# A block product in the second MLP matmul in place of DMA transposes of q and k

## The chip, the cores and the metric

The kernel runs on one core of a Trainium2 chip. A core has a matrix engine (TensorE, PE in the profile; its weight loads are listed apart as PEld), three engines for elementwise work (VectorE = DVE, ScalarE = ACT, GpSimd = POOL), a queue engine that only issues transfers (SyncE = SP), 16 DMA engines, an on-chip memory of 128 partitions (SBUF) and a small accumulator memory in which matmuls put their results (PSUM). Every engine works through its own list of instructions in order; engines wait for each other through semaphores. The metric is the device time of one execution in microseconds; several executions are taken and their median is given. The profile is one of these executions.

## The reference

Local attention with a few global keys and a linear bias on distance, then the real part of a two-dimensional Fourier transform added to its input, a normalisation, and a two-layer MLP added again:

```python
scores = scale * np.matmul(q, k.transpose(0, 1, 3, 2)) + bias      # B=4, H=8, S=768, D=64
scores = np.where(keep, scores, -1e9)                              # local 96, global 8
a = softmax(scores)
x = heads_joined(np.matmul(a, v))                                  # (4, 768, 512)
mixed = np.real(np.fft.fft(np.fft.fft(x, axis=1), axis=2))
u = x + mixed
un = (u - mean(u)) / np.sqrt(var(u) + 1e-6)
ch = np.maximum(un @ w_ch1, 0.0) @ w_ch2                           # 512 -> 2048 -> 512
return u + ch
```

The inputs and the output are fp32. The kernel casts to fp16 for its matmuls.

## The kernel before

**Tiling.** Each batch has 768 rows of 512. Attention goes by head pairs, `n = 4 * b + hp`. After attention the rows of a batch are taken in six residues mod 6, and two residues (256 rows) form a chunk, so there are 12 chunks `c = 3 * b + pr`.

**Stages of one batch.**
1. `load` and `cast_qk` bring q, k of a head pair to SBUF (tiles `qs`; for the first head pairs `hT`) and cast them to fp16 (`qk`).
2. `trans` makes `qkT`, q and k with the head dimension on partitions. For batches 0 and 1 twelve TensorE transposes write a PSUM bank `pt` (L495) and DVE copies it out (L501). For batches 2 and 3 (`b >= XB`) `trans_dma` issues four transposes per head pair from the SP queue (L475); `cast_qk` lays out `qk` in two halves for it (L369, L371).
3. `score` (PSUM `sc`), exponentials on ACT (`er`, L555), the mask product on DVE (`ex`, L570), `av` (`pav`, L662) and its normalisation on DVE (`x`, L681 and L682).
4. `bounce` writes `x` to DRAM and reads it back with rows regrouped (`xr`). Beside it `fold_s` and `fold_d` on DVE (L725 to L794) form sums and differences, which save matmuls in the Fourier transform: this is called the fold below.
5. `y_unit` (PSUM `py`, L814 and L817, copied to `zy`), `mirror` on POOL (`rev`, `ww`), `u_unit` (PSUM `pu`, L895; DVE adds `xr` to make `u`, L914), normalised `un` (L929, L931), and `nt_unit`, which transposes it (`ptu`, L959) into `unT` (L967, L969). From `py` to the first MLP matmul is called the passage below.

**The MLP of one chunk.** `ph_unit` makes a pair of 128-wide blocks of the hidden layer: eight matmuls of 256 columns (L987), and a relu by ACT or DVE into `hT` (L993, L994). There are eight such units to a chunk; `hT` has 16 blocks of 256 rows. `pg_unit` multiplies with `w2`: for each of two row blocks `t`, 16 matmuls of 512 columns (L1010) into one bank `pg`, in four parts of four. DVE multiplies by the row's inverse deviation, adds `u` and writes a tile `ob` (L1021), which SP stores (L1026).

**What sets the order.** The builder has a planner, `Plan`, which keeps a clock per engine and emits instructions one after the other. Elementwise work is announced with the engines that may do it, an estimated duration and what it needs. Four streams feed TensorE: `MIX` (stage 5), `ATT` (stages 2 and 3), `PH` and `PG`. `Plan.run` takes the unit that can start first by its estimates, looking ten units ahead in `MIX` and `ATT` and one ahead in `PH` and `PG`. Once built, the order on each engine is fixed. Numbers of buffers are in `NBUF`; a unit waits until its buffer or its PSUM bank is free. Attention and stage 5 share two double banks (`xx`), the MLP has two banks `ph` and two `pg`.

```python
        pl.run([(MIX, True), (ATT, True), (PH, False), (PG, False)])
```

Of the kernel before, what the change touches and what calls it, by code (L numbers as in the profile page):

```python
# [14 lines left out]
P = 128  # L15


class Plan:
# [7 lines left out]
    SEM = 0.06  # L26
    LAT = {"ACT": 0.14, "DVE": 0.12, "POOL": 0.08}

    def __init__(self):
        self.t = {"PE": 0.0, "ACT": 0.0, "DVE": 0.0, "POOL": 0.0, "SP": 0.7, "DMA": 1.9, "DMA2": 0.0}  # L30
        self.tok = {}
        self.ready = []
        self.pending = []
        self.rings = {}
        self.left = {}
        self.n = 0
# [49 lines left out]
    def emit(self, place):  # L86
# [6 lines left out]
        if dma:  # L93
            q = "DMA2" if eng == "ACT" else "DMA"
            end = self.t[q] = max(self.t[q], end) + dma
        else:
            lat += self.LAT.get(eng, 0.0)
# [4 lines left out]
        if ring is not None:  # L102
            self.rings[ring].append(end + lat)
# [4 lines left out]
    def pe(self, us, after=0.0):  # L108
        end = self.t["PE"] = max(self.t["PE"], after) + us
        return end + 0.15  # L110
# [48 lines left out]
def act(n):  # L159
    return 0.06 + n / 1200.0  # L160


def dve(n):
    return 0.085 + n / 960.0


def dve2(n):
    return 0.075 + n / 1920.0
# [7 lines left out]
def kernel(  # L176
# [23 lines left out]
    XB = 2  # L200
# [59 lines left out]
    def bank(tag, name, dtype=FP32):  # L260
# [4 lines left out]
        if "late" not in early:  # L265
# [5 lines left out]
    NBUF = {"hT": 3, "vs": 2, "qk": 2, "qs": 3, "qkT": 4, "er": 2, "eg": 1, "x": 1, "xr": 1, "zy": 1, "eA": 1,  # L271
            "ww": 1, "rev0": 1, "u": 4, "un": 2, "unT": 2, "ob": 2}
# [19 lines left out]
    w2 = kon.tile([P, NJ, Dm], FP16, tag="w2", name="w2")  # L292
# [15 lines left out]
    TT = {}  # L308

    def load(b, hp, which):  # L310
# [5 lines left out]
        if which == "v" and b == 0:  # L316
# [4 lines left out]
            pl.later([("SP", 0.45, run)], free(vtag, vi), 0.0, [("ld", "v", n)], lat=1.7, dma=1.6)  # L321
        elif which == "v":
# [6 lines left out]
            pl.later([("SP", 0.9, run)], free(vtag, vi) + gate, 0.0, [("ld", "v", n)], lat=1.7, dma=2.67)  # L329
        elif b == 0 and hp < 3:  # L330
            cell = {}

            def run(cell=cell):
                cell[0] = buf("hT", hp, [P, 2, NS, 2 * Dh], FP32, 2)
                for w, src in enumerate((q, k)):
                    qk_dma(cell[0][:, w], src, b, h0)
            pl.later([("SP", 0.9, run)], free("hT", hp), 0.0, [("ld", "qk", n, w) for w in range(2)], lat=1.7, dma=3.2)
            for w in range(2):
                cast_qk(b, hp, w, lambda w=w, cell=cell: cell[0][:, w], ("hT", hp))
        else:  # L340
            for w, src in enumerate((q, k)):
                cell = {}
                i = 2 * (n - 3) + w
# [4 lines left out]
                pl.later([("SP", 0.45, run)], free("qs", i) + gate, 0.0, [("ld", "qk", n, w)], lat=1.7, dma=1.6)  # L348
# [6 lines left out]
    def cast_qk(b, hp, w, src, freed):  # L355
        n = HP * b + hp

        def cast(on):
            if n not in qk16:
                qk16[n] = buf("qk", n, [P, 2, NS, 2, Dh] if b < XB else [P, 2, 2, NP, 2, Dh], FP16, 1)  # L360
            if b < XB:
                d = qk16[n][:, w]
                s = src().rearrange("p (h i) (t d) -> p h (i t) d", h=2, t=2).rearrange("p h j d -> p j h d")
            else:
                for t in range(2):
                    d = qk16[n][:, t, w]
                    s = src().rearrange("p (h i) (t d) -> p t i h d", h=2, t=2)[:, t]
                    if on == "ACT":
                        A(d, s, AF.Copy)  # L369
                    else:  # L370
                        nc.gpsimd.tensor_copy(d, s)  # L371
                return
# [81 lines left out]
    def kg_copies(b, hp):  # L454
        n = HP * b + hp
        for s in range(2):
            def cp(s=s):
                c0 = 16 * (hp % 2) + 8 * s
                nc.gpsimd.tensor_copy(
                    kG[b % 2][64 * s:64 * s + 64, hp, c0:c0 + NG].rearrange("p (j m) -> p j m", j=2),  # L460
                    TT[n][64 * s:64 * s + 64, 1, 0:P].rearrange("p (j m) -> p j m", j=2)[:, :, 0:NG // 2])
            pl.later([("POOL", 0.2, cp)], [("qkT", n)] + ([("gldone", b - 2, hp // 2)] if b > 1 else []), 0.0,
                     [("kG", n, s)], [("free", "qkT", n)], rank=RA(b))

    def trans_dma(b, hp):
        n = HP * b + hp
        done = []

        def xb(a, t):
            if not done:  # L470
                TT[n] = buf("qkT", n, [P, 2, S], FP16, 6)
            done.append(1)
            o = TT[n].rearrange("p w (i a t m) -> p a t (w i) m", a=2, t=2, m=64)[:, a, t]
            i = qk16[n][64 * a:64 * a + 64, t].rearrange("p w i h d -> p (w i h d)")
            nc.sync.dma_start_transpose(o, i)  # L475
        at = [(a, t) for a in range(2) for t in range(2)]
        for x, (a, t) in enumerate(at):
            pl.later([("SP", 1.3, lambda a=a, t=t: xb(a, t))],
                     ([("qk", n, 0), ("qk", n, 1)] + free("qkT", n)) if x == 0 else [("xb", n, x - 1)], 0.0,
                     [("xb", n, x)], lat=0.0, dma=0.01)  # L480
        pl.later([("SP", 0.0, lambda: None)], [("xb", n, 3)], 0.0, [("qkT", n)], [("free", "qk", n)], lat=2.2, dma=0.5)
        kg_copies(b, hp)

    def trans(b, hp):
        if b >= XB:
            return trans_dma(b, hp)
        n = HP * b + hp

        def run(start, ring):
# [17 lines left out]
            kg_copies(b, hp)  # L507
# [128 lines left out]
    def av(b, part, jp):  # L636
# [8 lines left out]
        def run(start, ring):  # L645
# [31 lines left out]
            def norm():  # L677
                if b not in X:
                    X[b] = buf("x", b, [P, NS, Dm], FP16, 4 if b else 5)
# [4 lines left out]
            pl.later([("DVE", 0.09 + dve(128 * nh), norm)], free("x", b), e, [("x", b, hp, jp) for hp in part], CD(b),  # L684
# [6 lines left out]
    def bounce(b):  # L691

        on, eng = ("ACT", nc.scalar) if b else ("SP", nc.sync)
        for half in range(2):
            def wr(half=half):
# [4 lines left out]
                for t in range(2):  # L700
                    eng.dma_start(rows[t], X[b][64 * t:64 * t + 64, :, c])
            pl.later([(on, 1.2, wr)], [("x", b, hp, jp) for hp in (2 * half, 2 * half + 1) for jp in range(NP)] + [("xw", b, 0)][:half], 0.0,
                     [("xw", b, half)], [("free", "x", b)], lat=1.7, dma=2.4 if b else 1.5)

        def rd():
            XR[b] = buf("xr", b, [P, NS, Dm], FP16, 3)
            rows = XD[b].rearrange("(m r) d -> m r d", r=6)
            eng.dma_start(XR[b], rows)
        pl.later([(on, 0.5, rd)], [("xw", b, 0), ("xw", b, 1)] + free("xr", b), 0.0, [("xr", b)], lat=1.7, dma=3.8 if b else 2.4)

    def fold_s(b):
# [3 lines left out]
        for n, (c0, cw) in enumerate(parts):  # L715
# [25 lines left out]
            def f4(c0=c0, cw=cw, cell=cell):  # L741
# [7 lines left out]
                     [("f1", b, n)], [("free", "x", b)] * (2 if len(hps) == HP else 1))  # L749
# [19 lines left out]
    def fold_d(b, needs):  # L769
# [30 lines left out]
        pl.later([("DVE", 0.95 + 1.0, g1)], needs + free("eA", ia) + free("ww", IW(b, NA(b))), 0.0, [("w", b, 0)])  # L800
# [83 lines left out]
    def u_unit(b, pr):  # L884
# [4 lines left out]
        def run(start, ring):  # L889
# [20 lines left out]
            def add():  # L910
                u = UT[c] = buf("u", HP + c, [P, 2, Dm], FP32, 2)
                sm = MV[c] = wk.tile([P, 2, 4], FP32, tag="sm", name=f"sm_{c}", bufs=6)
                for a, rr in enumerate((r0, r1)):
# [5 lines left out]
            pl.later([("DVE", 2 * dve(512) + 0.25, add)], [("xr", b)] + free("u", HP + c), e, [("u", c)],  # L919
                     [("free", "xr", b)] + CD(b), ring=ring)  # L920
# [11 lines left out]
            for a in range(2):  # L932
                pl.later([("ACT", 0.52, lambda a=a: un("ACT", a)), ("DVE", 0.38, lambda a=a: un("DVE", a))],
# [5 lines left out]
            for a in range(2):  # L939
                pl.later([("ACT", 0.62, lambda a=a: square(a))],  # L940
# [36 lines left out]
    def ph_unit(c, jp):  # L977
        needs = [("unT", c), ("w1", jp // 2)] + (free("hT", 3 + c) if jp == 0 else []) + [("CD",)]

        def run(start, ring):  # L980
            if jp == 0:
                HT[c] = buf("hT", 3 + c, [P, NJ, CH], FP16, 2)
# [14 lines left out]

    GP = {}

    def pg_unit(c, t, part):  # L1000
        b, pr = divmod(c, NP)
        rs = PAIRS[pr][t]
        needs = [("h", c, 2 * part), ("h", c, 2 * part + 1), ("w2", part)]

        def run(start, ring):
            if part == 0:
                GP[0] = bank("pg", f"pg_{c}_{t}")
            pg = GP[0]
# [193 lines left out]
```

## Time and profile before

| | |
|---|---|
| median of three runs | 290.23 us (288.24 to 290.87) |
| the profiled execution | 288.24 us, its span 286.4 us |
| mean granted TensorE clock | 0.976 |
| PE busy | 254.1 us (89%), 2340 matmuls |
| DVE busy | 172.2 us (60%), 367 instructions |
| ACT busy | 146.6 us (51%), 247 instructions |
| POOL busy | 53.4 us (19%) |
| chain that ended last | PE 74%, DVE 16%, DMA 3%, ACT 2%, SP queue 2% |
| `ph` matmuls L987 | 768, 94.4 us busy |
| `pg` matmuls L1010 | 384, 91.1 us busy |
| DMA transposes L475 | 32 issues of 1.25 us (median), 3.3 us to landing, between 94.8 and 177.2 us |
| loads of `w2` L1099 | four, issued between 68.7 and 73.6 us, 10.8 us to landing |

How to read it: busy time is the union of an engine's instructions. Matmuls overlap and their ends are modelled, so one matmul of 256 columns lasts 273 ns in the list while the next begins after 0.11 us. In a list of groups a row gives line, engine, operation, output and inputs, shapes and count, then busy time and mean duration, then the engine's idle time before the group and who ended it. In a timeline the columns are start, duration, engine, line, operation, and in brackets the idle time before it with its releaser. In a table of stretches, each engine's busy time is followed by its count of instructions, and after POOL come the granted clock, the DMA share and GB/s.

### The profile page before, as it was taken

The page shows a single profiled execution, that of the slowest core. Times are in us where ns is not written, and L with a number is a line of the kernel's source. Part 1 is how long each engine was busy: PE and PEld are TensorE (multiplying, and loading weights), DVE is VectorE, ACT ScalarE, POOL GpSimd, SP SyncE. Part 2 cuts the span into 40 slices and gives each one's busy share as a digit, 9 for nine tenths or more (in the row PEclk, how much of TensorE's full clock was granted, in tenths as well). Part 3 has the DMA queues.
Part 4 walks back from the last instruction along what each step waited for, and adds up shares of the span by engine and source line. Part 5 has one row for each costly group of instructions (what it writes and reads, how often), then busy time and mean ns, then how long its engine had stood idle before and what let it go on. Part 6 is the DMA issues. An engine that isn't in the chain of part 4 may idle for free.

```text
span 286.4 us, 5852 instructions
## 1 busy us (share of the span) xinstructions
PE 254.1 (89%) x2340; PEld 168.4 (59%) x2340; DVE 172.2 (60%) x367; ACT 146.6 (51%) x247; POOL 53.4 (19%) x122
## 2 busy tenths in 40 slices
PE   1899348899997499999999999699999999999993
PEld 1344236688654267666566446568877677757441
DVE  3247996756679956187158985886895735211121
ACT  2667913999761228378392265589334336324000
POOL 1337004316401061331101004030002120100000
PEclk9999958999999799999999999999999999999999
DMA  7997969999999998839566995100242010010111
GB/s 216 286 295 92 192 129 262 202 199 199 194 208 267 240 258 162 152 108 207 130 180 156 178 277 110 41 3 0 57 108 96 37 39 38 2 73 11 64 73 74
DMA packets 75691, 40.19 MB, mean 140 GB/s; under 512 B 33680, under 2 KB 71824, under 8 KB 75664
## 3 DMA queue, kind: packets, MB, share of 16 engines
q1 hardware_dynamic: 66208, 30.91, 45.4%
q0 software_dynamic: 4224, 4.19, 9.5%
q10 hardware_dynamic: 5232, 4.72, 6.8%
q8 instruction: 18, 0.29, 0.5%
q14 instruction: 9, 0.07, 0.1%
HBM read 31.42 MB, written 9.44 MB: 143 GB/s over the span
## 4 chain that ended last, share of the span: by engine, by line
PE 74%; DVE 16%; DMA 3%; ACT 2%; SPq 2%; issue 1%; POOL 1%; ACTq 0%; DVEq 0%; POOLq 0%
PE ph L987 30%; PE pg L1010 23%; PE sc L532 5%; DVE x L682 3%; DVE u L914 3%; PE py L814 3%; PE pu L895 2%; PE pt L495 2%; PE py L817 2%; PE pav L662 2%; DMA qkT<-qk 1%; DMA ident<-idm 1%; SPq L475 1%; PE ptu L959 1%; PE sc L527 1%
## 5 line engine op out<-in xcount | busy, mean ns | idle before, releaser
L987 PE MATMUL ph<-unT,w 128*128 128x256 f16 x768 | 94.4, 273 | 0.2 <-DVE unT L969 0.2
L1010 PE MATMUL pg<-w,hT 128*128 128x512 f16 x384 | 91.1, 380 | 0.0
L987 PEld LDWEIGHTS <-w 128*128 128x128 f16 x768 | 72.1, 98 | 17.7 <-issue 5.9
L993 ACT ACTIVATE hT<-ph 128x512 f16<-128x512 f32 x60 | 35.8, 597 | 46.0 <-PE ph L987 46.0
L1010 PEld LDWEIGHTS <-hT 128*128 128x128 f16 x384 | 36.5, 98 | 36.0 <-issue 1.3
L1021 DVE SCALAR_TENSOR_TENSOR ob<-pg,sm,u 128x512 f32<-128x512 f32 x24 | 18.0, 748 | 49.6 <-PE pg L1010 48.1
L994 DVE TENSOR_SCALAR hT<-ph 128x512 f16<-128x512 f32 x36 | 24.9, 690 | 17.1 <-PE ph L987 16.8
L555 ACT ACTIVATE er<-sc 128x992 f16<-128x992 f32 (+2 forms) x36 | 32.4, 921 | 2.2 <-PE sc L532 2.0
L570 DVE TENSOR_TENSOR ex<-er,mk 128x992 f16<-128x992 f16 (+2 forms) x36 | 22.6, 635 | 6.1 <-ACT er L555 5.9
L814 PE MATMUL py<-t,ww 128*128 128x256 f16 x48 | 13.2, 327 | 13.1 <-DVE ww L779 13.1
L369 ACT ACTIVATE qk<-qs 128x384 f16<-128x384 f32 x30 | 13.6, 514 | 20.3 <-DVE ww L780 8.0
L863 POOL COPY ww<-zy 128x512 f16<-128x512 f16 x16 | 9.3, 610 | 64.4 <-DVE zy L832 36.0
L532 PE MATMUL sc<-qkT 64*128 64x256 f16 (+1 forms) x192 | 17.7, 273 | 1.6 <-ACT qkT L505 0.7
L929 ACT ACTIVATE un<-u,sm 128x512 f16<-128x512 f32 x15 | 10.5, 717 | 15.5 <-DVE sm L918 15.4
L914 DVE SCALAR_TENSOR_TENSOR u<-pu,xr 128x512 f32<-128x512 f32 x24 | 15.6, 687 | 4.0 <-PE pu L895 3.3
L682 DVE TENSOR_TENSOR x<-pav,rc 128x512 f16<-128x512 f32 (+1 forms) x27 | 17.1, 632 | 0.9
L662 PEld LDWEIGHTS <-ex 128*128 128x128 f16 x352 | 15.2, 97 | 3.1 <-issue 1.1
L662 PE MATMUL pav<-v,ex 128*128 128x65 f16 x352 | 16.4, 193 | 0.5 <-DVE x L682 0.4
L830 ACT ACTIVATE zy<-py 128x1024 f16<-128x1024 f32 (+1 forms) x11 | 9.0, 827 | 14.2 <-PE py L817 10.7
L938 ACT ACTIVATE un<-un 128x512 f16<-128x512 f16 x24 | 14.8, 620 | 1.3 <-PE ptu L959 1.3
L532 PEld LDWEIGHTS <-qkT 64*128 64x128 f16 x192 | 6.2, 95 | 15.0 <-issue 11.2
L814 PEld LDWEIGHTS <-ww 128*128 128x128 f16 x48 | 5.6, 116 | 15.8 <-DVE ww L779 13.7
(95 smaller groups left out, 282.6 us busy)
## 6 DMA issues: line engine op xcount, KB each, us to landing
out_dram<-ob SPq DMA_DIRECT2D x24, 256.0 KB, 2.2
qs<-in_q_dram SPq DMA_DIRECT2D x13, 384.0 KB, 6.3
qs<-in_k_dram SPq DMA_DIRECT2D x13, 384.0 KB, 6.4
vs<-in_v_dram SPq DMA_DIRECT2D x24, 192.0 KB, 6.2
w<-in_moe_w_ch_dram POOLq DMA_DIRECT2D x8, 512.0 KB, 10.8
xd<-x ACTq DMA_DIRECT2D x12, 192.0 KB, 4.2
xr<-xd ACTq DMA_DIRECT2D x3, 768.0 KB, 4.5
u<-in_v_dram SPq DMA_DIRECT2D x4, 384.0 KB, 6.2
```

What stands on the lines that cost most here:

```text
L532: nc.tensor.matmul(pa[:, s, c0:c0 + cw], TT[n][lo:lo + 64, 1, i * P:(i + 1) * P], TT[n][lo:lo + 64, 0, i * P:i * P + cw], start=(b > 0), s ...
L555: A(mine(), cut(pa), AF.Exp, 0.0, 0.125)
L570: VT(o, mine(), m, op=ALU.mult)
L662: nc.tensor.matmul(po[:, jj, hh * 65:(hh + 1) * 65], lhsT, v16[b % 2][:, i, h, 0:65], start=(jp == 0 and a == 0), stop=(a == len(ops) - 1) ...
L682: VT(X[b][:, 2 * jp:2 * jp + 2, first * Dh:(first + nh) * Dh].rearrange("p j (h d) -> p j h d", d=Dh), pv[:, :, :, 0:Dh], rc.to_broadcast( ...
L814: nc.tensor.matmul(o, wr, t1_sb[:, rs, 128:384], start=True, stop=(wi is None))
L914: V.scalar_tensor_tensor(u[:, a].rearrange("p (n r) -> p n r", r=4), pu[:, a].rearrange("p (r n) -> p n r", r=4), 1.0, XR[b][:, rr].rearra ...
L987: nc.tensor.matmul(ph[:, a * CH:(a + 1) * CH], w1[:, d, jb * P:(jb + 1) * P], UNT[c][:, d, :], start=(d == 0), stop=(d == ND - 1))
L993: pl.later([("ACT", act(512), lambda: A(dst, ph, AF.Relu)), ("DVE", dve(512), lambda: V.tensor_scalar_max(dst, ph, 0.0))], [], e, [("h", c ...
L994: ("DVE", dve(512), lambda: V.tensor_scalar_max(dst, ph, 0.0))],
L1010: nc.tensor.matmul(pg, HT[c][:, jb, t * P:(t + 1) * P], w2[:, jb, :], start=(jb == 0), stop=(jb == NJ - 1))
L1021: V.scalar_tensor_tensor(cell[0], pg, MV[c][:, t, 3:4], UT[c][:, t, :], op0=ALU.mult, op1=ALU.add)
```

## The change

Two things are exchanged, and the buffers and the planner's numbers with them.

**Transposes.** `XB`, `trans_dma` and the split layout of `qk` go; all 16 head pairs are transposed on TensorE and copied by DVE.

**Second product.** For each chunk, `hT` (256 rows by 2048) and `w2` (2048 by 512) are cut in two along each axis. The 2 by 2 block product is made from seven products of blocks in place of eight (eight matmuls of 256 columns each). The block sums of `w2` are made once (`w2_sums`), those of `hT` for each chunk (`s_sums`), all on VectorE, some of them in place. The products go to two banks, A and D, in five steps; after each step VectorE multiplies by the inverse deviation and adds the bank to `u`, and the next step continues on the bank (matmuls with no start flag). `u` is stored when all are added; `ob` goes.

**Buffers.** `hT` 3 to 2, `qs` 3 to 2, `ob` gone; `x` and `xr` share one buffer; four buffers `sx` and a constant tile `w2t` are new; `w2` shares a tile with q and k of the third and fourth head pairs. The planner's estimates differ throughout.

```diff
-    SEM = 0.06
-    LAT = {"ACT": 0.14, "DVE": 0.12, "POOL": 0.08}
+    SEM = 0.1
...
-        return end + 0.15
+        return end + 0.06
...
 def act(n):
-    return 0.06 + n / 1200.0
+    return 0.19 + n / 1200.0
 def dve(n):
-    return 0.085 + n / 960.0
+    return 0.15 + n / 960.0
 def dve2(n):
-    return 0.075 + n / 1920.0
+    return 0.16 + n / 1920.0
...
-    NBUF = {"hT": 3, "vs": 2, "qk": 2, "qs": 3, "qkT": 4, "er": 2, "eg": 1, "x": 1, "xr": 1, "zy": 1, "eA": 1,
-            "ww": 1, "rev0": 1, "u": 4, "un": 2, "unT": 2, "ob": 2}
+    NBUF = {"hT": 2, "vs": 2, "qk": 2, "qs": 2, "qkT": 4, "er": 2, "eg": 1, "x": 1, "zy": 1, "eA": 1,
+            "ww": 1, "rev0": 1, "u": 4, "un": 2, "unT": 2, "w2": 1, "sx": 4}
...
     def trans(b, hp):
-        if b >= XB:
-            return trans_dma(b, hp)
...
-    def pg_unit(c, t, part):
...
+    def w2_sums(i):
+        def run():
...
+            VT(w2t[:, 1, k0, :], b22, b12, op=ALU.subtract)
+            VT(b12, b12, b11, op=ALU.subtract)
+            VT(w2t[:, 0, k0, :], b22, b12, op=ALU.subtract)
+            VT(w2t[:, 2, k0, :], b21, w2t[:, 0, k0, :], op=ALU.subtract)
+        pl.later([("DVE", 4 * dve2(1024), run)], [("w2", i), ("w2", 2 + i)], 0.0, [("w2t", i)], rank=1)
+
+    def s_sums(c):
...
+        def s1():
+            VT(new(0), block(1, 0), block(1, 1), op=ALU.add)
+        def s3():
+            VT(block(1, 0), block(0, 0), block(1, 0), op=ALU.subtract)
+        def s2():
+            VT(new(1), SX[c, 0], block(0, 0), op=ALU.subtract)
+        def s4():
+            VT(new(2), block(0, 1), SX[c, 1], op=ALU.subtract)
...
+    def pg_units(c):
...
+        def prod(o, lhs, rhs, first, last=True):
+            for j in range(NK):
+                nc.tensor.matmul(o, lhs(j), rhs(j), start=(first and j == 0), stop=(j == NK - 1), skip_group_check=True)
...
+        def p1(start, ring):
+            A_ = GP[c, "A"] = bank("pg", f"pgA_{c}")
+            prod(A_[:, 0:HC], a(0, 0), bw(0, 0), True)
...
+            pl.later([("DVE", dve(HC), lambda: stt(u(0)[:, 0:HC], A_[:, 0:HC], 0, u(0)[:, 0:HC]))],
+                     [("rstd", c)], e, [("ra", c, 0)], rank=0)
+
+        def p45(start, ring):
+            D_ = GP[c, "D"] = bank("pg", f"pgD_{c}")
+            prod(D_[:, 0:HC], a(1, 1), tw(2), True)
+            prod(D_[:, HC:Dm], sx(0), bw(0, 1), True)
...
+            pl.later([("DVE", dve(Dm), lambda: stt(u(1), D_, 1, u(1)))],
+                     [("rstd", c)], e, [("rd", c, 0)], rank=0)
+
+        def p6(start, ring):
+            prod(A_[:, 0:HC], sx(1), tw(0), False)
...
+            pl.later([("DVE", dve(HC), lambda: stt(u(0)[:, HC:Dm], A_[:, 0:HC], 0, u(0)[:, HC:Dm]))],
+                     [], e, [("ra", c, 1)], rank=0)
+
+        def p32(start, ring):
+            prod(D_[:, HC:Dm], sx(2), bw(1, 1), False)
+            prod(D_[:, 0:HC], a(0, 1), bw(1, 0), True)
...
+            pl.later([("DVE", dve(Dm), lambda: stt(u(0), D_, 0, u(0)))],
+                     [("ra", c, 1)], e, [("ob", c, 0)], ring="pg", rank=0)
+
+        def p7(start, ring):
+            prod(A_[:, 0:HC], a(1, 0), tw(1), False)
...
+            def last():
+                o = u(1).rearrange("p (x n) -> p x n", x=2)
+                stt(o, A_[:, 0:HC].unsqueeze(1).to_broadcast([P, 2, HC]), 1, o)
+            pl.later([("DVE", dve(Dm), last)], [("rd", c, 0)], e, [("ob", c, 1)], ring="pg", rank=0)
+
+        PG.append((h0 + ws, ("pg",), p1))
+        PG.append((h1 + [("s", c, 1)], ("pg",), p45))
+        PG.append(([("s", c, 2), ("ra", c, 0)], None, p6))
+        PG.append(([("s", c, 4), ("rd", c, 0)], None, p32))
+        PG.append(([("s", c, 3), ("ra", c, 1)], None, p7))
```

## The prediction

> **What bounds the kernel now.** The page's slices come first.
>
> ```profile
> PE   1899348899997499999999999699999999999993
> DVE  3247996756679956187158985886895735211121
> PEclk9999958999999799999999999999999999999999
> ```
>
> A digit covers 7.2 us. TensorE (PE) is full except at the start, in slices 5 and 6 (36 to 50 us) and in slice 13 (93 to 100 us), where DVE stands at 9 and the granted clock drops to 7. Next, busy time by stretches that I cut at the first `py` matmul of each batch and at the first `ph` matmul after it; the columns are PE, weight loads, DVE, ACT, POOL, then clock.
>
> ```profile
> 39.80:52.20 12.40, 9.85 (x88) 7.36 (x89) 9.26 (x26) 5.61 (x10) 3.07 (x7) 0.78 0.84 195
> 88.10:97.10 9.00, 3.67 (x24) 1.53 (x21) 8.76 (x16) 0.94 (x2) 0.96 (x1) 0.96 1.13 260
> 97.10:110.90 13.80, 13.69 (x117) 9.00 (x118) 10.48 (x23) 6.52 (x10) 4.62 (x9) 0.90 0.95 211
> 184.60:214.90 30.30, 30.30 (x335) 23.69 (x335) 24.22 (x45) 19.50 (x35) 3.29 (x6) 1.00 0.16 40
> ```
>
> Each batch has a fold (DVE sums after attention, before `py`) and a passage (`py`, copies, `pu`, sums for `u`, normalising, `ptu`, then `ph`). Both are latency chains. Where `pg` matmuls of earlier chunks lie beside them PE stays full (13.69 of 13.80); where none do it does not. The timeline shows such a gap, and what ended it:
>
> ```profile
> 88.13 3.62 PE L1010 MATMUL pg<-w,hT 128*128 128x512 f16 x16
> 97.07 0.39 PE L814 MATMUL py<-t,ww 128*128 128x256 f16 x1 [5.33 <-DVE ww L779]
> ```
>
> The prices come from the groups, shapes kept apart, and from the chain in order of time (start, us, what):
>
> ```profile
> L1010 PE MATMUL pg<-w,hT 128*128 128x512 f16 x384 | 91.1, 380 | 0.0
> L1021 DVE SCALAR_TENSOR_TENSOR ob<-pg,sm,u 128x512 f32<-128x512 f32 x24 | 18.0, 748 | 49.6 <-PE pg L1010 48.1 <-issue 1.5
> L501 DVE COPY qkT<-pt 128x1536 f16<-128x1536 f16 x7 | 6.7, 953 | 2.9 <-PE pt L495 2.9
> L731 DVE TENSOR_TENSOR ww<-eA 128x1024 f16<-128x1024 f16 x3 | 2.1, 688 | 0.2
> ```
> ```profile
> 70.35 0.67 PE pt L495 x12
> ...
> 230.45 1.75 PE ph L987 x16
> 232.20 0.86 PE pg L1010 x4
> ```
>
> Matmuls overlap, so the chain gives their real spacing: 0.109 us for 256 columns, 0.215 for 512, 0.67 for twelve transposes. So PE is the bound, and `pg` is the cover that keeps it busy.
>
> **PE work.** Removed: 384 x 0.215 = 82.6. Added: 12 chunks x 7 products x 8 matmuls = 672 of 256 columns, each with its own weight load exactly like `ph`: 672 x 0.109 = 73.2. Eight transposes come back to PE: 8 x 0.67 = 5.4. Net -4.0 us.
>
> **DVE work.** 48 sums of 1024 fp16 elements and eight for the weights: 56 x 0.688 = 38.5. Sixty accumulations replace 24: 36 of 512 elements at 0.748 and 24 of 256. No fp32 row has 256 elements; the `zy` rows of L743 fall from 681 ns (512) to 415 (256), and the same 0.27 off 748 gives 0.48: 26.9 + 11.5 - 18.0 = +20.4. Eight `qkT` copies: 8 x 0.953 = 7.6. Together +66.5 on 172.2, so about 239 of a 286 us span.
>
> **Queues.** SP loses 32 transposes of 1.25 us each and the loads behind them move up. I give that nothing: between 150 and 170 us, where transposes hold up the scores, PE was still 97% busy, so at most 0.5 us lies there. ACT and POOL cast the same elements in one piece (836 ns) instead of two (2 x 514); ACT is off the path. Storing from `u` keeps the last store's tail: 282.1 to 286.4, 4.3 us.
>
> **What moves.** The built order of the changed program decides. Buffers for `hT` fall from three to two, and the five product steps of a chunk are ordered so that every chunk at hand is finished before `py`. Before, 28, 24 and 36 `pg` matmuls lie in the passages of batches 1, 2 and 3 (6.0, 5.2 and 7.7 us); afterwards one product of 0.87 us remains in each of the first two and 2.6 us in the third. I walk the stretches, PE by its spacings, DVE by start-to-start times (sum 0.61, accumulation 0.75 or 0.48).
>
> Start to `py` of batch 0: 39.8, unchanged. Passage 0: 12.4, plus 1.1 because `pt_4` now stands ahead of the first `ph` and waits for a cast ending near 52.5: 13.5.
>
> First attention stretch (sixteen `ph` units and three more, chunk 0's products, scores, transposes, `pav`): 38.7 of PE work. New wait: chunk 0's first product needs the eight weight sums, which in DVE's order stand behind the first normalisation of `pav` for batch 1. PE has only `pt_7` (0.67) to do meanwhile: 0.2 + 0.7 + 8 x 0.69 - 0.67 = 5.8. Behind that product on PE stand scores and `pav`, on which softmax and the fold wait. It would cost 0 had DVE run ahead, but it cannot pass the normalisation; more if `w2` lands late (last issue 73.6 before, landing 8 to 13 us later). I take 5.8: 44.5.
>
> Folds. The fold alone takes DVE 9.9 (89.3 to 99.2). In batch 1 the queue up to chunk 2's last sum also holds one relu (0.6), four long and four short accumulations (4.9) and four sums (2.4): 17.8. The product that needs this sum (1.74) stands ahead of `py` on PE: 19.5, against 17.0 of PE work. Batch 2 is alike, with 0.9 of PE-DVE ping-pong, since each accumulation must empty its bank before the next product. I take 20 and 20. In batch 3 `py` stands behind the third product step and 10.6 of DVE, then 2.1 more: 13.
>
> Passages 1 to 3. Uncovered, 12.4 was measured (part at a low clock); covered, 13.8 to 15.5. Walking `py`, ACT copy, mirror, `pu`, 1.3 us of `u` sums per chunk and `ptu` gives 12.0 each. PE work in it: 24 x 0.109 for `py`, 2.7 `pu`, 0.9 `ptu`, 1.9 of products and scores: 8.1. So 4 us idle each.
>
> Attention stretches 2 and 3 have 38.7 of PE work each and 27 of DVE: I take 40. The end: 33.1 of PE, 1 of waits, 8.0 for the last chunk (7.0 of work, its sums in series with accumulations), 4.3 tail: 46.4.
>
> Sum: 39.8 + 13.5 + 44.5 + 20 + 12 + 40 + 20 + 12 + 40 + 13 + 12 + 46.4 = 313.2 span, against 286.4. The profiled execution took 288.24, 1.84 more than its span and 2.0 below the median: 315.0.
>
> **A rule beside a row.** After the 5.33 us gap `py` matmuls came 0.21 us apart until 98.9, then 0.11; after the gap of the first fold the clock was 0.78 to 50 us. The Trainium skill, "TensorE: Matmul & The Clock Gate", section "Part 1: The HAM clock gate", says that an idle window of about 3.4 us halves the clock until PE has again been busy that long. It speaks against this change, which opens gaps. The new gaps are in pieces of 1 to 2 us with work between, so my sum has none of it; a half-clock window in each of the three passages would, as an estimate from that page, lose 3 x 1.7 = 5 us and make it 320.
>
> **Rivals.**
> (a) Lost cover, as summed: 315. For it: 88.1 to 97.1 shows what a fold without `pg` does.
> (b) DVE becomes the bound everywhere. It carries 36.5 of 44.5 in the first stretch and 16 of 20 in the folds; relus that free `ph` banks queue behind sums. Against: 24.2 of 30.3 left PE full between 184.6 and 214.9. If the three attention stretches grow by a sixth, +20: 335; half of that, 325.
> (c) Folds run at PE's pace (17.0 + 15.3 + 12.2, saving 8.5) and the weight sums hide (5.8): 301.
> (d) Faster: the 4.0 us of PE work come off and cover stays: 284. It decides once new idle time is below 4 us in all. For it: PE is 74% of the chain. Against: the order leaves nothing to lay beside three passages.
> (e) The products don't get cheaper: at 94.4 / 768 = 0.123 us (the page's busy time of `ph`) 672 cost 82.6, no saving; +9.4: 324. Against: the chain's 1.75 for sixteen.
>
> **Numbers.** (a) 0.65, (b) 0.15, (c) 0.09, (d) 0.05, (e) 0.03, and 0.03 for gains and losses that cancel. Predicted 315. The range 301 to 329 takes in (c), (e) and half of (b); outside are (d), no change and the upper half of (b). A measurement can tell about 1% here: faster 0.05, same 0.03, slower 0.92.
>
> **What would show it.** PE work near 250 with a span over 300; PE idle about 5 us just before the first product, ended by the weight sums; idle in each passage, ended by `u` sums and copies; `py` of batches 1 and 2 preceded by a product that waited for a DVE sum; transposes' SP time gone without the end moving. It is wrong if PE is full through the passages, if the weight sums are done before the first product, or if DVE, not PE's lack of work, ends most gaps in the attention stretches.

## The result and the profile after

The changed kernel takes 314.37 us (median of 4 runs, 312.40 to 316.37) beside 290.55 us for the kernel before in the same comparison: a ratio of 1.083, 95% interval 1.072 to 1.094. It is slower by 24 us. The profiled execution took 312.74 us, its span 311.0 us, at a mean granted clock of 0.937 (0.976 before). In this and the later table a median is over all runs of a kernel, while the ratio leaves out the few slow runs, more than 1.5% above the fastest of their kernel (one each of e3, e10 and the kernel before).

The slices of the page after; a digit covers 7.8 us:

```profile
PE   2798077993199987779999976789999987899994
DVE  3438979899648997588779996677788998762553
PEclk9799679997569998999999997999999999999998
```

Counted from 1 (the prediction counts from 0), TensorE was full before from slice 15 on, but for slice 26 (6 tenths) and the last. Now it has holes in slices 10 and 11 (70 to 86 us), 15 to 18 (109 to 140 us), 24 to 27 (179 to 210 us) and 33 to 35 (249 to 272 us). VectorE, at 1 or 2 tenths in the last six slices before, is at 6 to 9 from slice 18 to slice 36. The clock sinks in slices 10 to 12.

The same in stretches, cut at the first `py` of each batch, at the first `ph` after it and at the first fold instruction of VectorE. Columns as before: stretch, its length, PE, weight loads, DVE, ACT and POOL busy with counts, granted clock, DMA share, GB/s.

```profile
39.78:52.35 12.57, 9.77 (x100) 7.47 (x101) 10.46 (x27) 6.68 (x12) 3.84 (x8) 0.87 0.78 149
52.35:103.20 50.85, 39.19 (x428) 30.71 (x425) 39.50 (x64) 25.41 (x41) 18.56 (x29) 0.83 1.09 200
103.20:124.07 20.87, 17.43 (x157) 14.68 (x155) 18.75 (x33) 5.24 (x8) 2.81 (x6) 0.94 0.92 232
124.07:136.65 12.58, 8.89 (x105) 7.25 (x104) 8.14 (x21) 6.82 (x8) 3.06 (x7) 0.96 0.12 43
136.65:172.69 36.04, 36.04 (x423) 28.87 (x421) 29.63 (x53) 23.04 (x41) 5.07 (x11) 1.00 0.25 71
172.69:192.49 19.80, 15.80 (x140) 13.12 (x138) 18.33 (x32) 3.98 (x6) 1.91 (x5) 0.93 0.41 128
192.49:205.00 12.51, 8.82 (x105) 7.22 (x104) 8.14 (x21) 6.82 (x8) 3.06 (x7) 0.97 0.11 42
205.00:240.91 35.91, 35.91 (x418) 28.72 (x416) 29.05 (x52) 20.99 (x39) 4.08 (x10) 1.00 0.09 28
240.91:252.80 11.89, 11.38 (x104) 9.82 (x102) 11.57 (x21) 2.29 (x4) 0.00 (x0) 1.00 0.45 143
252.80:265.86 13.06, 9.24 (x104) 7.71 (x105) 11.77 (x29) 4.45 (x6) 3.07 (x7) 1.00 0.11 41
265.86:311.00 45.14, 40.74 (x376) 35.99 (x375) 22.48 (x37) 15.70 (x32) 2.64 (x6) 0.98 0.10 36
```

In the rows of 36 us, attention beside the MLP, TensorE is full at full clock (36.04 of 36.04). Time is lost in four kinds of place: the first attention stretch (11.7 us without PE work, clock 0.83), the first two folds (3.4 and 4.0 us), the three passages (3.7 to 3.8 us each), and the end (4.4 us, 4.0 of it the tail after the last matmul, which was 4.3 before).

Some of this was there already. The kernel before, cut in the same way, attention and fold in one row (the last row here is its third passage):

```profile
52.21:97.07 44.86, 38.53 (x424) 28.32 (x424) 33.44 (x57) 29.57 (x51) 13.30 (x25) 0.99 1.11 217
97.07:110.80 13.73, 13.62 (x117) 8.93 (x117) 10.51 (x23) 6.42 (x10) 4.62 (x9) 0.90 0.94 210
110.80:169.44 58.64, 58.12 (x501) 36.04 (x497) 37.05 (x69) 33.31 (x64) 8.30 (x23) 1.00 0.75 171
169.44:184.54 15.10, 12.77 (x122) 8.54 (x120) 10.87 (x27) 7.83 (x12) 3.75 (x11) 1.00 0.52 112
215.45:230.29 14.84, 14.84 (x133) 10.22 (x132) 9.34 (x22) 5.44 (x10) 3.76 (x9) 1.00 0.12 47
```

Its second passage had 2.33 us without PE work; the first and third had almost none (0.11 and 0.00). So from the end of passage 0 on, idle PE time grows by 8.8 us in the three passages (2.4 to 11.2), by 8.8 in the first attention stretch with its fold (6.3 to 15.1), by 3.5 in the second with its fold (0.5 to 4.0) and by 0.6 elsewhere: 21.6 of 24.5 us. The other 2.9 are PE busy time, which grew although 4.0 us of work were to go.

The timeline of TensorE names what ended the larger gaps (start, duration, line and tile, in brackets the gap and its releaser):

```profile
83.11 0.82 PE L455 MATMUL pt<-ident,qk 128*128 128x128 f16 x6 [7.92 <-ACT qk L366]
85.05 0.82 PE L455 MATMUL pt<-ident,qk 128*128 128x128 f16 x6 [1.12 <-ACT qk L366]
...
121.11 1.45 PE L1019 MATMUL pgD<-w,sx 128*128 128x256 f16 x8 [2.08 <-DVE sx L1005]
...
186.06 1.05 PE L1019 MATMUL pgA<-w2t,sx 128*128 128x256 f16 x8 [1.57 <-DVE sx L1002]
189.46 1.53 PE L1019 MATMUL pgD<-w,sx 128*128 128x256 f16 x8 [2.35 <-DVE sx L1005]
```

In both folds the product that stands ahead of `py` waits for the last block sum of its chunk. The timeline of VectorE shows the last weight sums, and then why that block sum is late in the first fold:

```profile
82.04 0.69 DVE L979 TENSOR_TENSOR w2t<-w 128x1024 f16<-128x1024 f16 x1 [2.36 <-DMA w<-in_moe_w_ch_dram]
...
84.22 0.69 DVE L982 TENSOR_TENSOR w2t<-w,w2t 128x1024 f16<-128x1024 f16 x1
...
103.20 0.96 DVE L692 TENSOR_TENSOR eA<-x 128x1536 f16<-128x1536 f16 x1
...
120.37 0.68 DVE L1005 TENSOR_TENSOR sx<-hT,sx 128x1024 f16<-128x1024 f16 x1
120.97 1.82 DVE L461 COPY qkT<-pt 128x1536 f16<-128x1536 f16 x2
```

From the fold's first instruction (103.20) to the end of that sum (120.37 + 0.68) 17.85 us pass, in which VectorE works through fold, relu, accumulations and sums with one pause of 0.73 us. Behind it come two `qkT` copies. Until they are done, `pt_8` and `pt_9` hold both `xx` banks, and `py` cannot have one. In this execution that was not the last wait: the copies end at 122.79, and `py` comes at 124.07, right behind the late product.

In the first stretch the chain of work that ended last gives another cause (start, us, what):

```profile
66.48 17.65 DMA qs<-in_k_dram
...
84.15 0.85 ACT qk L366
...
121.11 3.16 PE pgD L1019 x16
...
153.99 1.75 PE pgD L1019 x16
```

The load of k for the last head pair of batch 1 takes 17.65 us from issue to landing (the median of the page is 5.7), beside the four loads of `w2`; the load of q issued just before it takes 17.0. The first half of `pt_7` waits for the cast of q (the gap of 7.92 us), the second for that of k (1.12), and in TensorE's order the first product stands behind `pt_7`. The last row has sixteen matmuls of 256 columns in 1.75 us, 0.109 us each, as priced. The row before it has the same work in 3.16 us, after the gap of 2.08 us.

### The profile page after: what moved, and what is told of

It is laid out like the page before. It is cut to its first block, busy times and chain, and to the rows that moved or that the text cites. A ratio compares the mean times of both kernels' runs of the same rounds, so it can differ in the third digit from the quotient of the medians.

```text
span 311.0 us, 6644 instructions
## 1 busy us (share of the span) xinstructions
PE 255.5 (82%) x2724; PEld 204.1 (66%) x2724; DVE 232.3 (75%) x468; ACT 143.7 (46%) x228; POOL 59.6 (19%) x124
## 4 chain that ended last, share of the span: by engine, by line
PE 60%; DVE 24%; DMA 8%; ACT 3%; issue 2%; POOL 2%; SPq 1%; POOLq 0%; DVEq 0%
PE ph L954 25%; PE pgD L1019 11%; PE pgA L1019 7%; DMA qs<-in_k_dram 6%; DVE u L1037 4%; DVE u L881 4%; PE sc L499 3%; PE pt L455 3%; PE pav L629 3%; DMA u<-in_v_dram 2%; PE py L781 2%; DVE x L649 2%; ACT ex L525 2%; PE py L784 2%; DVE eA L744 1%
## 5 line engine op out<-in xcount | busy, mean ns | idle before, releaser
L1019 PEld LDWEIGHTS <-hT 128*128 128x128 f16 x384 | 39.0, 102 | 8.8 <-issue 3.0
L1019 PEld LDWEIGHTS <-sx 128*128 128x128 f16 x288 | 28.1, 100 | 12.6 <-DVE sx L1005 6.1
L1037 DVE SCALAR_TENSOR_TENSOR u<-pgD,sm,u 128x512 f32<-128x512 f32 x24 | 18.0, 748 | 17.9 <-PE pgD L1019 17.9
L1019 PE MATMUL pgD<-w,sx 128*128 128x256 f16 x192 | 26.7, 285 | 5.3 <-DVE sx L1005 5.3
L797 ACT ACTIVATE zy<-py 128x1024 f16<-128x1024 f32 (+1 forms) x12 | 10.2, 880 | 44.8 <-PE py L784 32.3
L1037 DVE SCALAR_TENSOR_TENSOR u<-pgA,sm,u 128x256 f32<-128x256 f32 (+1 forms) x36 | 20.3, 570 | 13.4 <-PE pgA L1019 13.1
L366 ACT ACTIVATE qk<-qs 128x768 f16<-128x768 f32 x20 | 16.6, 840 | 19.5 <-DMA qs<-in_q_dram 16.3
L455 PE MATMUL pt<-ident,qk 128*128 128x128 f16 x192 | 15.6, 241 | 9.2 <-ACT qk L366 9.0
L461 DVE COPY qkT<-pt 128x1536 f16<-128x1536 f16 x15 | 14.2, 955 | 9.1 <-PE pt L455 8.9
L455 PEld LDWEIGHTS <-qk 128*128 128x128 f16 x192 | 13.1, 108 | 10.8 <-ACT qk L366 9.5
L881 DVE SCALAR_TENSOR_TENSOR u<-pu,x 128x512 f32<-128x512 f32 x24 | 15.6, 688 | 3.8 <-PE pu L862 3.8
```

What stands on the lines that cost most here:

```text
L455: nc.tensor.transpose(o[:, j % 2], src[:, w, j].rearrange("p h d -> p (h d)"), idn)
L881: V.scalar_tensor_tensor(u[:, a].rearrange("p (n r) -> p n r", r=4), pu[:, a].rearrange("p (r n) -> p n r", r=4), 1.0, XR[b][:, rr].rearra ...
L1019: nc.tensor.matmul(o, lhs(j), rhs(j), start=(first and j == 0), stop=(j == NK - 1), skip_group_check=True)
L1037: V.scalar_tensor_tensor(o, x, r(t), acc, op0=ALU.mult, op1=ALU.add)
```

## The experiments

The runs e1 to e11 were timed beside the kernel before, whose median was 289.2 to 289.4 us in these comparisons. The changed kernel's ratio comes from the first comparison and is known to about 1%, so the differences between it and these runs are known to some 3 us.

| run | edit | median, us | ratio to before, 95% interval |
|---|---|---|---|
| changed kernel | | 314.37 | 1.083 (1.072 to 1.094) |
| e1 | before, transposes on TensorE | 289.58 | 0.998 (0.993 to 1.002) |
| e7 | e1, no `pg` left for the passages | 301.96 | 1.041 (1.035 to 1.048) |
| e2 | changed, transposes by DMA | 304.58 | 1.053 (1.045 to 1.061) |
| e3 | changed, without the 48 sums | 304.17 | 1.049 (1.041 to 1.058) |
| e4 | changed, `w2` loaded earlier | 303.20 | 1.049 (1.042 to 1.056) |
| e6 | changed, `qkT` copies ahead of the fold | 305.19 | 1.057 (1.050 to 1.065) |
| e5 | e6, products kept for the passages | 309.55 | 1.069 (1.063 to 1.075) |
| e8 | e6 and e2 | 303.89 | 1.050 (1.044 to 1.056) |
| e10 | e6, e2 and e4 | 303.01 | 1.044 (1.038 to 1.050) |
| e9 | e6 and e3 | 300.27 | 1.037 (1.033 to 1.042) |
| e11 | before, seven products in chunks 9 and 10 only | 288.25 | 0.998 (0.995 to 1.001) |

### The two halves of the change, each alone

e1 is the kernel before with one number changed:

```diff
-    XB = 2
+    XB = 4
```

> The kernel before with only the transposes of batches 2 and 3 moved to TensorE, the second product left as it was. Lost-cover theory: 5.4 us of matmuls come to a full PE, DVE's 7.6 us of copies find room: 294 to 298 us. If DVE's load is what made the change slow, the copies alone cost about an eighth of its 24 us plus the PE work or more: 298 to 304. If the transposes were the whole change: 310 or more.

289.58 us, no difference: the expectation of 294 and more missed. The windows of e1 around its second batch:

```profile
101.75:115.52 13.77, 13.77 (x133) 9.72 (x132) 11.14 (x25) 7.83 (x12) 5.69 (x13) 1.00 0.96 249
115.52:162.87 47.35, 47.35 (x483) 32.88 (x481) 36.30 (x68) 30.44 (x48) 7.14 (x16) 1.00 0.48 131
162.87:176.39 13.52, 13.52 (x125) 9.17 (x124) 9.21 (x20) 7.20 (x12) 3.82 (x9) 1.00 0.12 47
176.39:214.53 38.14, 38.14 (x375) 26.18 (x373) 27.93 (x52) 18.60 (x32) 3.01 (x8) 1.00 0.21 62
```

TensorE is full without a hole for 113 us, passages included, where the kernel before had some (12.77 of 15.10 in the passage of batch 2). PE busy rose by 7.3 us (254.1 to 261.4) and the span by 2.2 us. The Trainium skill, "VectorE: DVE Perf Modes", section "Rules for kernel authors", advises TensorE for a 128x128 transpose where the result may go to PSUM, and the DMA path otherwise; by time alone e1 shows no difference. So in the kernel before the eight transposes cost about what the DMA transposes had cost in waits (its idle PE time fell from 32.3 to 27.2 us). Alone they are no part of the loss, which comes only with the second product, its buffers, its estimates and its order.

e2 puts the other half back into the changed kernel:

```diff
+    XB = 2
...
     def trans(b, hp):
+        if b >= XB:
+            return trans_dma(b, hp)
```

> The changed kernel with the DMA transposes put back for batches 2 and 3. Lost-cover theory: the passages stay empty, PE gets 5.4 us lighter and DVE 7.6, mostly where other waits end later: 306 to 311 us. If the transposes' return is what cost the time: 292 to 298.

304.58 us, 10 us below the changed kernel and just under the range. The same transposes that cost nothing in e1 seem to cost 10 us here. Of the 9.2 us between the two profiled spans (311.0 and 301.8) 5.1 are PE busy time (255.5 to 250.4), about the 5.4 us of the transposes, and 4.1 are idle time. e6 asks about the idle part.

### Lost cover or VectorE?

e3 leaves the block sums of `hT` out and keeps TensorE's order:

```diff
         def s1():
-            VT(new(0), block(1, 0), block(1, 1), op=ALU.add)
+            new(0)
```

(and so for the other three).

> The changed kernel with the order on PE kept and the 48 block sums of the hidden layer left out (the products take plain blocks), so its output is not the reference's. 33 us of DVE work go, PE work stays. Lost-cover theory: only the waits for sums in three folds and at the end go (2.1 to 3 us each), the passages keep their idle time: 304 to 309 us. DVE-bound theory: most of the loss comes back: 290 to 299.

304.17 us: in the range of lost cover; the 290 to 299 of VectorE as the bound fell. 29 us of VectorE work taken away (48 x 0.61) return 10.

e7 asks the reverse: take the cover from a kernel that has the whole product and 66 us less VectorE work than the changed one (165.9 us busy).

```diff
+            if t == 1:
+                pl.tok[("pgd", c)] = e, "PE"
...
-        MIX.append(([("w", b, 0 if g in (0, 3) else 1)], BANKS(b), run))
+        MIX.append(([("w", b, 0 if g in (0, 3) else 1)] + ([("pgd", NP * b - 1)] if b else []), BANKS(b), run))
```

> The kernel before with all transposes on TensorE (as e1) and one more need: the first py of batches 1 to 3 waits until the last pg matmul of the batch before has been issued, so that no pg is left for the passages. Same instructions on every engine as e1, VectorE work unchanged, second product whole. Lost cover: passages of 12 to 13 us with 8 to 9 us of PE work, 3 x 4 us of new idle time, 299 to 303. If cover in the passages is worth nothing (PE can make it up later, and the changed kernel is slow for its VectorE work alone): 288 to 292.

301.96 us, 12.4 us above e1 and inside the range of lost cover. Its three passages:

```profile
120.35:132.15 11.80, 8.22 (x105) 6.81 (x104) 9.52 (x20) 7.26 (x11) 5.25 (x11) 1.00 0.50 149
...
190.83:201.77 10.94, 7.25 (x89) 6.00 (x88) 7.08 (x17) 7.02 (x10) 3.07 (x7) 1.00 0.06 24
...
244.32:254.25 9.93, 6.78 (x82) 5.52 (x80) 5.98 (x17) 5.97 (x8) 3.08 (x7) 1.00 0.07 26
```

3.6, 3.7 and 3.2 us without PE work, 10.4 in all, where e1 had none: holes of the size of those in the changed kernel's passages, with the same 2436 matmuls as e1 (the planner gave ACT 16 elementwise instructions that VectorE had in e1). So with the whole product an order that leaves nothing beside the passages costs about 12 us. In the changed kernel the same holes are 8.8 us more than the kernel before had.

### The rest of the loss: the banks and the queue on VectorE

e6 changes one rank, so that the `qkT` copies go ahead of the fold on VectorE:

```diff
-            ... e, [("qkT", n)], ring=ring, rank=RA(b))
+            ... e, [("qkT", n)], ring=ring, rank=0)
```

> The changed kernel with the rank of the qkT copies alone raised in front of the fold on VectorE (the other half of e5): the two xx banks come free for py and the scores of the next batch can start before py. Nothing is held back, all products of a chunk stay ahead of py. If banks held by waiting transposes, not the missing products, make the passages idle: 303 to 310, about as e5. If it is the missing products: 311 to 316, within 1% of the changed kernel, the fold being later by two copies of 0.95 us for each batch and the passages shorter by as much.

305.19 us, in the range for banks held by waiting transposes. But its windows show that the gain isn't in the first two passages:

```profile
125.86:138.21 12.35, 7.82 (x96) 6.28 (x96) 9.78 (x23) 6.44 (x9) 3.08 (x7) 1.00 0.12 43
138.21:192.35 54.14, 53.17 (x567) 43.58 (x565) 46.28 (x80) 26.54 (x47) 8.04 (x17) 0.97 0.27 79
192.35:204.17 11.82, 7.82 (x99) 6.29 (x97) 8.49 (x23) 7.09 (x10) 3.08 (x7) 1.00 0.12 44
204.17:242.95 38.78, 38.74 (x436) 32.45 (x434) 34.52 (x62) 19.67 (x38) 3.03 (x8) 1.00 0.19 56
242.95:258.00 15.05, 15.05 (x170) 13.74 (x168) 13.54 (x32) 6.29 (x8) 3.74 (x7) 1.00 0.10 36
```

The first two passages have their 4 us of idle still. Attention and fold of batch 2 have 53.17 of 54.14 us of PE work (before the edit 51.84 of 55.84), with scores of batch 3 in the fold, the first at 168.48 us; and the third passage is full, with 170 matmuls for 104, so that a part of this gain is cover too.

e5 adds to e6 what would bring cover back: products of chunks 2, 5 and 8 held until `py` has been issued.

```diff
+        if pr == 2 and b + 1 < B:
+            hs = hs + [("w", b + 1, 1)]
...
+        hold = [("y", b + 1, 2, 0)] if pr == 2 and b + 1 < B else []
+        h0 = [("h", c, jp) for jp in range(4)] + hold
```

> The changed kernel with one change of order: in batches 1 to 3 the products of chunks 2, 5 and 8 (their block sums too) are held back until the fold's weights are there and the first py groups have been issued, so that three to five of the seven products lie in each passage, and the qkT copies are no longer ranked behind the fold. Same matmuls, same VectorE work, same buffers. Lost cover (the idle time sits in passages with nothing to lay beside them): passages 1 and 2 hold about 4 us more PE work each and lose 3 to 4 us of idle each, 303 to 310 in all. VectorE as the bound: the same VectorE work only changes places, 311 to 318. A third possibility, that products in the passage push the fold's chain and the u sums back on VectorE by as much as they fill on TensorE: passages grow to 16 us or more and the total stays at 311 to 318 with PE busier in the passages.

309.55 us: within the numbers given for lost cover, but e6, which has the rank alone, takes 305.19, so that by the medians holding the products back costs 4.4 us. That is a miss for lost cover as I had put it. The first two passages did become full (the third has 2.23 us of idle); the hole moved to the fold ahead of them, 7.08 us in the first and 8.59 in the second (the second in windows, then its gap in the timeline):

```profile
138.15:192.44 54.29, 45.70 (x519) 36.98 (x517) 46.38 (x84) 25.47 (x44) 7.42 (x16) 0.95 0.27 84
192.44:206.87 14.43, 14.43 (x144) 12.39 (x144) 7.88 (x20) 8.58 (x12) 3.08 (x7) 0.85 0.05 19
```
```profile
192.44 0.37 PE L781 MATMUL py<-t,ww 128*128 128x256 f16 x1 [8.59 <-ACT er L522]
```

A gap of 8.59 us while VectorE worked through the fold (8.07 us busy), then the passage at a clock of 0.85. The products of a chunk are one stock of some 6 us: laid beside the passage, they are missing beside the fold.

e4 issues the loads of `w2` earlier:

```diff
-            needs = ... [("v", 1, HP - 1), ("free", "w2", 0)] if i == 4 else ...
+            needs = ... [("un", 0, 1), ("free", "w2", 0)] if i == 4 else ...
```

> The changed kernel with the four loads of the second weights issued after the first normalised chunk (about 51 us) instead of after the last v of batch 1 (63.7 us). If the 9.0 us gap before the first product comes from loads that collide with these weights and from the weight sums behind them, it shrinks to 2 or less: 305 to 309 us. If the bytes only move and other loads come late instead: 312 or more.

303.20 us, 11 us less, 2 under the range. The first gap fell from 7.92 to 1.29 us (its releaser is now the weight sums), yet `py` of batch 1 moved from 124.07 only to 122.67. In e4's timeline the wait has gone into the fold, where VectorE is busy 11.90 of the 12 us from 110 to 122:

```profile
116.95 0.59 PE L499 MATMUL sc<-qkT 64*128 64x256 f16 x4 [6.44 <-DVE qkT L461]
...
122.67 0.37 PE L781 MATMUL py<-t,ww 128*128 128x256 f16 x1 [3.40 <-DVE qkT L461]
```

The rest of e4's gain stands in the second batch: from the `ph` after the first passage to the `ph` after the second it takes 61.3 us in place of 68.4. The planner's order there is another one, and which part of it did that was not taken apart.

### Do the gains add?

e8 is e6 with the transposes by DMA (edits of e6 and e2 together), e10 is e8 with e4's edit, e9 is e6 with e3's.

> e6 (the changed kernel with the qkT copies ranked ahead of the fold, 305.2) and the transposes of the last two batches by the crossbar again, as in e2 (304.6). If both removed the same thing, the two xx banks held by waiting transposes: 302 to 306, no more than either alone. If the 5.4 us of transposes on TensorE and the 7.6 us of copies on VectorE are what e2 saved, the two add up: 294 to 298.

> e8 and the loads of w2 issued earlier as in e4 (303.2, 11 us below the changed kernel). If the gains of e2, e4 and e6 are independent it would reach 284 to 288; if they all shorten the same waits: 298 to 304; the passages without cover (12.5 us by e7) stay in any case, so lost cover says not below 296.

> e6 with the 48 block sums of hT left out (the second product's operands are then not the right ones; the same matmuls in the same order). The changed kernel lost 10 us when its sums were left out (e3). If those 10 us were the fold and the xx banks queued behind the sums, e6 has already most of it: 301 to 305. If VectorE's time as such costs, it comes off again: 293 to 297.

303.89 and 303.01 us, both in the ranges for shared waits: three edits that bring 9 to 11 us each alone bring 11 together. The waits are the same only in part. The 4.0 us of idle PE time in the second stretch and fold are 3.3 in e2, 0.0 in e4 and 1.0 in e6. The 15.1 us of the first stretch and fold are 13.0 in e2, 13.4 in e4, 15.4 in e6 and 8.4 in e10; but what e10 gains there it loses in the passage behind:

```profile
114.01:133.06 19.05, 11.80 (x96) 9.17 (x97) 10.44 (x26) 7.14 (x11) 8.00 (x18) 0.66 0.98 219
```

There it has 7.25 us of idle at a clock of 0.66, where e6 has 4.53 at 1.00, and in the second stretch and fold 4.63. So waits that one edit removes come back elsewhere when the next is added.

By the median neither e8 nor e10 comes below e7, the whole product without cover (1.041, 1.035 to 1.048); e10 cannot be told from it. Only e9, with less VectorE work, goes on to 300.27, between its two ranges and nearer to the first: beside the edit of e6, leaving the sums out still brings 5 of the 10 us that it brought in e3.

### Seven products where there is nothing to cover

e11 is the kernel before with the block product in chunks 9 and 10 alone, behind the last passage; the sums lie in tiles of the finished attention.

```diff
+            if FROM <= c < FROM + 2:
+                s_sums(c)
+                pg_units(c)
+                continue
             for t in range(2):
                 for part in range(4):
                     pg_unit(c, t, part)
```

> The kernel before, unchanged but for chunks 9 and 10, which take the block product of seven (weight sums and hT sums written into tiles that the last attention has left, the weight sums ranked last on VectorE); chunk 11 and all others keep the whole product. Chunks 9 and 10 lie behind the last passage, where VectorE is busy two tenths, so sums and accumulations are hidden: 2 x (32 x 0.215 - 56 x 0.109) = 1.55 us less TensorE work. Lost cover as the only price of the block product: 287.5 to 289, ratio 0.994 to 0.997. If the products cost more than they save even there (waits between products for the accumulation that empties their bank): 289.5 to 292.

288.25 us beside 289.26, a ratio of 0.9976 (0.9948 to 1.0005): as expected, but not to be told from no change. Its timeline has chunk 10 and the start of chunk 11 like this:

```profile
269.34 1.04 PE L1088 MATMUL pgA<-w,hT 128*128 128x256 f16 x8
270.35 1.03 PE L1088 MATMUL pgD<-ex,hT 128*128 128x256 f16 x8
...
275.85 7.07 PE L1010 MATMUL pg<-w,hT 128*128 128x512 f16 x32
```

Chunk 10 goes from 269.34 to 275.85: seven products in 6.51 us, 0.4 of it three short pauses, against 6.88 for a whole product (32 x 0.215). Behind the last passage PE busy time is 50.6 us for 51.8 before, 1.2 less where 1.55 were forecast. The saving can be seen on TensorE; the time of the kernel is too coarse to show it.

## Why the prediction was right, step by step

**The total.** 315.0 against 314.37 in the median, a span of 313.2 against 311.0. That the total came so close is luck: two steps were off by far more than the total, in opposite directions (6.4 us too little, 8.0 too much). Besides, the sum adds 1.84 us to the span and leaves out the 2.0 us from the profiled execution to the median, which stand beside it; with them it gives 317.

| stretch | predicted | measured |
|---|---|---|
| to `py` of batch 0 | 39.8 | 39.8 |
| passage 0 | 13.5 | 12.6 |
| first attention stretch | 44.5 | 50.9 |
| fold 1 | 20 | 20.9 |
| passage 1 | 12 | 12.6 |
| second attention stretch | 40 | 36.0 |
| fold 2 | 20 | 19.8 |
| passage 2 | 12 | 12.5 |
| third attention stretch | 40 | 35.9 |
| fold 3 | 13 | 11.9 |
| passage 3 | 12 | 13.1 |
| end | 46.4 | 45.1 |

**Right in place and size.** The queue of the first fold (17.8 predicted, 17.85 measured), the product behind it ahead of `py`, and the passages, with nearly 4 us of idle each (in them waits for `zy`, `u` and `unT` end the gaps, as foreseen). The accumulation of 256 columns, for which there was no row, has a mean of 481 ns (0.48 taken). VectorE's total came out at 232.3 for 239. The tail after the last matmul measured 4.0 us for 4.3.

**Misread: the kernel before.** The lowest digits of TensorE early on (3 and 4) stand for 28.6 to 43 us, not for 36 to 50, and the 6 tenths at 179 to 186 us were passed over. They are in its second passage: the 24 `pg` matmuls there end at 178.7 us, and 2.3 us of idle follow. So the passages before were not all covered to their end, and of the 12 us of idle that the sum has in the new ones, 2.4 were there already.

**Wrong: the 5.8 us wait of the first stretch.** I took it for the wait of the first product for the weight sums, and named late landing of `w2` as the condition for more. The trace has 9.0 us in two gaps (7.92 and 1.12), 1.2 at `pav` ahead of them and some 1.4 at scores and `pvg`, and their releasers are the casts of q and k, whose loads took 17.0 and 17.65 us. The weight sums themselves waited until 82.04 for the second half of `w2` and were done at 84.9 (84.22 + 0.69), so they would have held the product until then too: two late arrivals, the second half of `w2` and the k of `pt_7`, either of which is enough. e4 shows that removing this alone moves the wait into the fold.

**Wrong: no half clock.** That the sum "has none of it" failed. From 85.05 to 90.90 TensorE ran at 0.50 after the large gap, and at 0.58 and 0.57 in the products after the gaps of 2.08 and 2.35 us ahead of `py`:

```profile
85.05:90.90 5.85, 5.85 (x30) 4.09 (x30) 1.44 (x2) 0.00 (x0) 1.96 (x4) 0.50 1.13 222
...
121.11:124.07 2.96, 2.96 (x17) 2.12 (x18) 1.68 (x2) 0.00 (x0) 0.74 (x4) 0.58 0.20 77
...
186.06:187.10 1.04, 1.04 (x8) 0.70 (x8) 1.04 (x2) 0.00 (x0) 0.00 (x0) 1.00 0.11 41
189.46:192.49 3.03, 3.03 (x16) 2.23 (x17) 1.68 (x2) 0.00 (x0) 0.74 (x4) 0.57 0.03 5
```

That is 5.85 / 2 = 2.9 us in the first stretch, 2.96 - 1.74 = 1.2 and 3.03 - 1.74 = 1.3 at the folds, 5.4 in all. The Trainium skill, "TensorE: Matmul & The Clock Gate", section "Part 1: The HAM clock gate", gave the prediction's side estimate of 5 us for three windows of 1.7 us. The sum comes near, but not its pieces (2.9, 1.2 and 1.3), nor the place, the passages (their clock is 0.96, 0.97 and 1.00). The page asks for an idle window of about 3.4 us; here half clock followed gaps of 2.08 and 2.35 us, but not the gap of 1.57 us, and in e5 not one of 2.23 us that ended at 252.24 us (clock 1.00 in the 3 us behind it). The length of the gap alone does not decide it in these runs.

**Wrong: 40 us for the later attention stretches.** PE work there is 36 us, not 38.7, which was the first stretch's count, and the 1.3 us of waits added to it did not come: 8 us too much, against 6.4 too little in the first stretch.

**The cause was a part of what I said.** Rival (a) was the likeliest, and e7 shows its price in the old product: 12.4 us beside e1. In the changed kernel the passages hold 8.8 us of the 21.6 of new idle time. Most of the rest lies at the late loads of the first stretch and in the first two folds, behind VectorE's queue with the last sum in it. A further 5.4 us of PE busy time went to half clock. One of e2, e3, e4 or e6 brings back 9 to 11 us, and those that were run together (e8, e9, e10) do not add up. My steps for the transposes (5.4 us on PE, 7.6 on DVE) and for the freed queue (nothing) gave 5.4 us of work and no wait: e1 as a whole shows no loss, since idle time fell by 5.1 us, and in the changed kernel e2 brings 5.1 us of PE busy time and 4.1 of idle. That the two banks held by waiting transposes make part of this idle time is argued from e6, where a rank alone brings 9 us, and from e2 and e6, which do not add in e8; it was not shown apart from the queue on VectorE. I had read from the order that nearly all the products stand ahead of `py`; I had not asked who holds the banks that `py` needs.

**The rivals.** (b), VectorE the bound everywhere, is false: the second and third attention stretches are full on TensorE with VectorE at 29.6 of 36.0 and 29.1 of 35.9, and without the 48 sums e3 still takes 304. It is the bound in the folds (18.75 of 20.87). (c) is false by the waits for `sx`. (d) needed less than 4 us of new idle; there were 21.6. (e) is false by 1.75 us for sixteen matmuls. Lost cover as the whole story is false too: e5 brought products back into the passages and won nothing over e6, and only 8.8 us of the new idle time are in the passages.

**Open.** How the loss outside the passages divides between the late sum, the held banks and the first stretch wasn't separated; with one of them gone the others take its place. Whether a planner with other estimates would find an order for seven products that covers folds and passages both wasn't tried.

## What to carry to other kernels

Work taken off a full engine is worth its time only where it wasn't covering someone else's chain: before replacing matmuls by fewer matmuls with sums around them, list what each of them lies beside, and look at the engine that gets the sums in just those stretches. A product that pays nothing in the dense part can be tried where no chain is left, as in the last chunks, and there e11 saved 0.37 us in a chunk of 6.88 us, too little to show in the kernel's time. When several single edits each bring the same gain, run them together before adding them up.

## What the runs showed of the hardware

- A gap of 2.08 us on TensorE, with the clock at 1.00 before and through it, was followed by 3 us at a mean clock of 0.58; a gap of 1.57 us was not, and in e5 neither was one of 2.23 us (clock 1.00 in the 3 us behind it). After gaps of 7.92 and 1.12 us the half clock lasted 5.85 us of full work.
- Beside four loads of `w2` of 512 KB on the GpSimd queue, a load of k of 384 KB on the SP queue took 17.65 us from issue to landing, one of q 17.0; with the `w2` loads issued earlier (e4), the median of the loads of k between 60 and 90 us was 3.9 us.
- In the mixed kernel, accumulating matmuls of 256 columns had a mean of 272 to 273 ns with operands from `hT`, from sums and from either weight tile: where the block sums lie made no difference to TensorE.
